# Forward transforms of two of four convolutions in three reduced-precision passes, with x loaded in a second order

## The chip, the cores and the metric

The kernel runs on one core of a Trainium2 chip. The metric is the device time of one execution in microseconds; the time before is the median of three runs. A core has five engines, each of which takes its instructions in order: TensorE (PE, with its weight loads as PEld), VectorE (DVE), ScalarE (ACT), GpSimd (POOL) and SyncE (SP). SP and POOL also issue transfers (DMA). Engines wait for each other through semaphores.

## The reference

2048 tokens of width D = 576 pass through two residual halves. `sa, ca, ga, sb, cb, gb` are the six parts of a modulation computed from a condition vector.

```python
h = _layernorm(x, axis=-1) * (1 + ca) + sa
x = x + ga * _A_ref(h, ...)          # long convolution along the tokens
h = _layernorm(x, axis=-1) * (1 + cb) + sb
x = x + gb * (relu(h @ w1) @ w2)     # w1: 576 x 4608, w2: 4608 x 576
```

`_A_ref` builds a convolution kernel K of 2048 steps for each of the 576 channels from 128 complex exponentials, convolves h with it by way of a Fourier transform, and adds `h * D_skip`. All inputs and outputs are float32.

## The kernel before

**Segments and blocks.** The tokens are cut into four segments of 512, s = 0 to 3. For each segment the kernel runs a convolution `conv(s)` and then a block of the feed-forward layer, block b = s. A block has 36 steps g of 128 hidden columns; over the kernel g counts from 0 to 143. One g is `first` (L1368, 14 matmuls of 128x512 into `hps`), the relu and its split on ScalarE and VectorE (`hh` at L1373, `hl` at L1374), and `second` (L1394, 14 matmuls into five `acc` tiles). These matmuls are in three passes over high and low parts: operands are fp32r, a float32 of reduced precision, and each product is high by high, high by low and low by high. `hh` and `xh` are high parts, `hl` and `xl` low parts; the weights are split the same way (L1333, L1343).

**Interleaving.** `conv(s+1)` is a generator that is advanced while block s runs: block 1 (g = 36 to 71) carries the last part of the convolution kernel's generation (`kps` at L521, evicted to `ker` at L531) and then conv(2); block 2 (g = 72 to 107) carries the end of block 1's output and conv(3). `step` (L1534) is called in the middle of every `first` and `second` and takes from the generator until the work done, in estimated microseconds, reaches a target that rises by `rate(b)` a call (L1706), with at most 7.0 in four calls and at most two matmul groups in one. A scheduler then fixes the order on every engine, and `Kept` marks instructions that stay in program order.

**A convolution.** conv(s) loads x of its segment (`x2`, four tokens in each partition, partition m holding tokens 4m to 4m+3), normalises it into `h` (`norm1`, L925: eight statistics on VectorE at L903, four aggregations at L912, four square roots on ScalarE at L913, then two VectorE operations a quarter at L937 and L938), and loads the kernel rows `kt` in two halves p. `mm_K(p)` and `mm_U(p)` are the first step of the forward transforms of kernel and input: `transform` (L845) makes eight fp32 matmuls of 128x128 by 128x288 each (`ps_f`, L854) with a table of cosines and sines as stationary operand, and evicts each on ScalarE (L855, `Z`). In conv(1) to conv(3) `ps_f` has one PSUM buffer. Butterflies on VectorE (L868 to L882) finish the transform; products with the spectra of earlier segments (L1034 to L1040), an inverse transform (L1061) and the addition to `x2` (L1066) follow. There are two tables because the kernel rows lie in another order: `fcK` has row j for position 8(j mod 16) + floor(j/16), `fcU` has row j for position j. conv(1) to conv(3) each have 32 `ps_f`.

**Transfers.** x, kt, the spectra (`Ua`, `Ka`, `R`) and the output's stores go by POOL's queue; the weights and the kernel rows' stores by SP's. Tiles called `S` (seven buffers) hold spectra, `h` and intermediate results; tiles called `T` (two buffers) hold half of one.

Of the kernel before, what the change touches and what calls it, by code (L numbers as in the profile page):

```python
# [18 lines left out]
P = 128  # L19
L = 2048  # L20
D = 576
# [8 lines left out]
PC = 288  # L30
# [21 lines left out]
class KGen:  # L52
# [10 lines left out]
    def v(self, out, a, b, op):  # L63
        self.tc.keep_in_program_order(self.nc.vector.tensor_tensor(out, a, b, op=op))  # L64
# [511 lines left out]
class Body:  # L576
# [34 lines left out]
    def early(self, kg):  # L611

        nc, I, sm = self.nc, self.I, self.sm
        x2 = self.x2[0] = self.x2p[0].tile([P, 4, D], F32, tag="x2", bufs=1, name="x2_0")
        nc.sync.dma_start(out=x2, in_=I["x"][0:512, :].rearrange("(m n) d -> m n d", n=4))
        self.fcU, self.fcK, self.gc = (
            sm.tile([P, 4, 2, P], F32, name=n) for n in ("fcU", "fcK", "gc")
        )
        for t, n in ((self.fcK, "fck"), (self.fcU, "fcu"), (self.gc, "gc")):
            nc.sync.dma_start(out=t, in_=I[n])  # L620
        kept = self.tc.keep_in_program_order
        self.mv1 = mv = sm.tile([P, 4, 5], F32, name="mv1")
        for i in range(4):
            yield
            st = sm.tile([P, 2, 6], F32, tag="st", bufs=8, name="st0")
            for p in range(2):
                kept(nc.vector.bn_stats(out=st[:, p], in_=x2[:, i, p * PC : (p + 1) * PC]))
            kept(nc.vector.bn_aggr(out=mv[:, i, 0:2], in_=st))
        yield
        kept(nc.scalar.activation(mv[:, :, 2], mv[:, :, 1], AF.Sqrt, bias=self.eps))  # L630
# [310 lines left out]
    def conv(self, s):  # L941

        nc = self.nc
        v = self.vec.tensor_tensor
        xp = self.xp[s % 2]
        if s:
            x2 = self.x2p[s % 2].tile([P, 4, D], F32, tag="x2", bufs=1, name=f"x2_{s}")
            self.x2[s] = x2
            Kept(self.tc, nc.gpsimd).dma_start(
                out=x2,  # L950
                in_=self.I["x"][s * 512 : (s + 1) * 512, :].rearrange("(m n) d -> m n d", n=4),
            )
        else:
            x2, h = self.x2[0], self.h0
            self.fcKn, self.gcn = (
                self.cv.tile([P, 4, P], F32, name=n) for n in ("fcKn", "gcn")
            )
            for t, a in zip((self.fcKn, self.gcn), self.I["neg"]):
                nc.gpsimd.dma_start(out=t, in_=a)
# [4 lines left out]

        kt = [kernel_tile(0) if s else self.kt0, None]
        yield -1 if s else "mod"
        if s:
            h = self.spec(f"h_{s}").rearrange("p a b c -> p a (b c)")
        hv = h.rearrange("m n (dd p q) -> m n dd p q", dd=4, p=2)

        def mm_U(p, Z):
            return self.transform(lambda n2: hv[:, n2, :, p], self.fcU, Z, s == 0)

        def mm_K(p, Z):
            ktv = kt[p].rearrange("p (t dd g) q -> p t dd g q", t=2, g=2)
            if s == 0 and p == 1:
                self.skip(kt[p], p, Kept(self.tc, nc.gpsimd))
            src = lambda n2: ktv[:, n2 // 2, :, n2 % 2]
            if s == 0 and p == 1:
                return self.transform1(src, self.fcK, self.fcKn, Z)  # L980
            return self.transform(src, self.fcK, Z, s == 0)
# [112 lines left out]
            yield from mm_K(1, ZK)  # L1094
            self.save(self.Rd[0][0], Ks[0], Kept(self.tc, nc.gpsimd))
        else:
            yield from both(self.norm1(x2, h), mm_K(0, ZK))
            kt[1] = kernel_tile(1)
            ZU = self.spec("Z")
            yield from both(spec_K(0, ZK), mm_U(0, ZU))  # L1100
# [603 lines left out]
            yield  # L1704

    def rate(self, b):  # L1706
        return (2.15, 1.8, 1.4, 0.5)[b]


def after(n, g):  # L1710
# [6 lines left out]
def both(a, b):  # L1717

    while True:
        n = 0  # L1720
        for g in (a, b):
            for w in g:
                n = 1
                yield w
                break
        if not n:
            return
# [62 lines left out]
```

## Time and profile before

| | |
|---|---|
| median of three runs | 1320.32 us (1318.6 to 1320.47) |
| the profiled execution | 1324.17 us, span 1322.4 us |
| mean granted TensorE clock | 0.943 |
| TensorE matmuls busy | 1210.1 us, 92% of the span |
| VectorE busy | 993.3 us, 75% |
| ScalarE busy | 518.8 us, 39% |
| GpSimd busy | 161.1 us, 12% |
| matmuls `ps_f` at L854 | 240 records, 80.2 us |
| chain of waits | PE 71%, DVE 16%, DMA 7% |

Busy times are summed over instructions of an engine, where overlaps count once. In the groups, "x128" is a count, "mean ns" the time of one. Matmuls are pipelined, so a matmul's record is longer than the distance to the next one's start; the cost of one in a run of many is read from the starts. An fp32 matmul of L854 appears as two records. "[2.69 <-ACT ker L531]" behind a row means that the engine was idle for 2.69 us before it and what released it. The clock is the part of full speed that was granted to TensorE.

### The profile page before, as it was taken

The page shows a single profiled execution, that of the slowest core. Times are in us where ns is not written, and L with a number is a line of the kernel's source. Part 1 is how long each engine was busy: PE and PEld are TensorE (multiplying, and loading weights), DVE is VectorE, ACT ScalarE, POOL GpSimd, SP SyncE. Part 2 cuts the span into 40 slices and gives each one's busy share as a digit, 9 for nine tenths or more (in the row PEclk, how much of TensorE's full clock was granted, in tenths as well). Part 3 has the DMA queues.
Part 4 walks back from the last instruction along what each step waited for, and adds up shares of the span by engine and source line. Part 5 has one row for each costly group of instructions (what it writes and reads, how often), then busy time and mean ns, then how long its engine had stood idle before and what let it go on. Part 6 is the DMA issues. An engine that isn't in the chain of part 4 may idle for free.

```text
span 1322.4 us, 27077 instructions
## 1 busy us (share of the span) xinstructions
PE 1210.1 (92%) x11094; PEld 973.6 (74%) x11094; DVE 993.3 (75%) x1538; ACT 518.8 (39%) x902; POOL 161.1 (12%) x256
## 2 busy tenths in 40 slices
PE   4665586899989998999999999999999999999998
PEld 3454464677767787787677887887888888998997
DVE  7899988999986999689468995467997237555543
ACT  5788423222223422622243225433222365434431
POOL 1676411011000100110001000100000000000000
PEclk9556787999989999999899999999999999999999
DMA  9758972988878967799779995877996658666641
GB/s 273 269 201 307 327 275 79 351 289 321 312 267 294 344 228 274 249 405 343 251 266 340 348 353 155 274 220 263 373 388 191 180 166 256 190 190 190 193 142 63
DMA packets 118032, 343.81 MB, mean 260 GB/s; under 512 B 17772, under 2 KB 21652, under 8 KB 107156
## 3 DMA queue, kind: packets, MB, share of 16 engines
q1 hardware_dynamic: 101332, 226.04, 51.0%
q0 software_dynamic: 16064, 114.67, 22.9%
q8 instruction: 87, 1.43, 0.4%
q10 hardware_dynamic: 512, 1.38, 0.3%
q14 instruction: 37, 0.30, 0.1%
HBM read 260.63 MB, written 81.40 MB: 259 GB/s over the span
## 4 chain that ended last, share of the span: by engine, by line
PE 71%; DVE 16%; DMA 7%; issue 3%; ACT 1%; POOL 1%; SPq 0%; ACTq 0%; DVEq 0%
PE acc L1394 28%; PE hps L1368 21%; PE hps L1495 7%; PE ps_f L854 5%; DMA L1d<-w 4%; PE kps L73 2%; PE kps L521 2%; PE ps_i L1061 2%; PE ph L73 2%; DVE T L486 1%; DVE W1r L488 1%; DMA x<-in_x_dram 1%; DVE Y L1040 1%; DVE T L64 1%; DVE w L1338 1%
## 5 line engine op out<-in xcount | busy, mean ns | idle before, releaser
L1394 PE MATMUL acc<-w,hh 128*128 128x512 f32 x1008 | 323.1, 403 | 3.2 <-ACT hh L1373 2.7
L1368 PE MATMUL hps<-xh,w 128*128 128x512 f32 x880 | 307.4, 410 | 0.7 <-ACT xh L49 0.7
L1394 PEld LDWEIGHTS acc<-w,hh 128*128 128x128 f32 x1008 | 187.4, 188 | 44.0 <-ACT hh L1373 3.6
L1368 PEld LDWEIGHTS hps<-xh,w 128*128 128x128 f32 x880 | 168.6, 192 | 38.7 <-ACT xh L49 1.3
L1394 PE MATMUL acc<-w,hl 128*128 128x512 f32 x504 | 195.1, 401 | 1.5 <-DVE hl L1374 1.5
L1343 ACT ACTIVATE w<-r 128x576 fp32r<-128x576 f32 x141 | 96.6, 685 | 229.7 <-PE acc L1394 195.2
L1368 PE MATMUL hps<-xl,w 128*128 128x512 f32 x440 | 175.7, 400 | 0.0
L1373 ACT ACTIVATE hh<-hps 128x512 fp32r<-128x512 f32 x110 | 65.7, 597 | 242.1 <-PE hps L1368 237.4
L1374 DVE SCALAR_TENSOR_TENSOR hl<-hps,hh 128x512 fp32r<-128x512 f32 x110 | 75.4, 685 | 113.1 <-ACT hh L1373 112.5
L1394 PEld LDWEIGHTS acc<-w,hl 128*128 128x128 f32 x504 | 94.3, 189 | 22.8 <-DVE hl L1374 3.0
L1333 ACT ACTIVATE w<-r 128x640 fp32r<-128x640 f32 x124 | 90.8, 732 | 42.7 <-DMA L1d<-w 42.1
L1368 PEld LDWEIGHTS hps<-xl,w 128*128 128x128 f32 x440 | 84.1, 191 | 18.3 <-DVE xl L49 0.4
L1040 DVE TENSOR_TENSOR Y<-Y,T 128x1152 f32<-128x1152 f32 x60 | 79.3, 1348 | 0.0
L73 PE MATMUL kps<-W,W 128*32 128x16 f32 x2304 | 39.4, 210 | 42.8 <-POOL W L70 28.4
L1368 PE MATMUL hps<-xs,w 128*128 128x512 f32 x220 | 78.0, 421 | 0.0
L855 ACT ACTIVATE Z<-ps_f 128x288 f32<-128x288 f32 x120 | 49.0, 410 | 71.6 <-PE ps_f L854 69.7
L73 PEld LDWEIGHTS kps<-W,W 128*32 128x32 f32 x2304 | 34.7, 142 | 56.4 <-POOL W L70 31.0
L521 PEld LDWEIGHTS kps<-W1r,W2r 128*32 128x32 f32 x3456 | 45.1, 113 | 38.8 <-issue 20.8
L521 PE MATMUL kps<-W1r,W2r 128*32 128x48 f32 (+2 forms) x3456 | 52.4, 202 | 15.9 <-ACT ker L531 9.3
L1503 DVE TENSOR_TENSOR C<-C,hps 128x256 f32<-128x256 f32 x17 | 7.1, 420 | 63.0 <-PE hps L1495 63.0
L1394 PE MATMUL acc<-hh,w 128*128 128x512 f32 x126 | 50.7, 402 | 0.0
L1394 PE MATMUL acc<-hl,w 128*128 128x512 f32 x126 | 49.9, 396 | 0.0
(307 smaller groups left out, 2197.9 us busy)
## 6 DMA issues: line engine op xcount, KB each, us to landing
r<-in_w_dram SPq DMA_DIRECT2D x144, 320.0 KB, 3.9
r<-in_w_dram SPq DMA_DIRECT2D x144, 288.0 KB, 4.9
w<-L2d SPq DMA_DIRECT2D x108, 288.0 KB, 4.1
w<-L1d SPq DMA_DIRECT2D x92, 320.0 KB, 3.9
W2r<-W2d POOLq DMA_DIRECT2D x18, 1536.0 KB, 8.5
W2d<-W SPq DMA_DIRECT2D x12, 1536.0 KB, 8.5
Ua<-Ud POOLq DMA_DIRECT2D x15, 1152.0 KB, 9.5
W<-W1d POOLq DMA_DIRECT2D x18, 768.0 KB, 9.4
```

The lines of the kernel that those rows point to most:

```text
L73: self.tc.keep_in_program_order(self.nc.tensor.matmul(*args, **kw))
L521: nc.tensor.matmul(ps[32 * dd : 32 * dd + 32, q, :], W2[:, r, ch], W1[:, r, ch], start=(r == 0), stop=(r == 1),)
L854: nc.tensor.matmul(o, fc[:, n2, c, :], src(n2), start=True, stop=True)
L855: ev = nc.scalar.activation(Z[:, n2, c], ps[:, :PC], AF.Copy)
L1040: v(y, y, T, op=op or ALU.add)
L1333: copy(g - 1)(w1[g][:, 0], r1[g], AF.Copy)
L1343: copy(g)(w[:, 0:D], r2[g], AF.Copy)
L1368: nc.tensor.matmul(ps, a, x, start=(i == 0), stop=(i == 13))
L1373: nc.scalar.activation(hh, ps, AF.Relu)
L1374: nc.vector.scalar_tensor_tensor(hl, ps, 0.0, hh, op0=ALU.max, op1=ALU.subtract)
L1394: nc.tensor.matmul(acc[i], a, x, start=(f == 0 and seen[i] == 1), stop=(f == NF - 1 and seen[i] == (3 if i < 4 else 2)),)
L1495: nc.tensor.matmul(out, l, m, start=(i == 0), stop=(i == len(ops) - 1))
```

## The change

For s = 2 and 3 the first step of the forward transforms is done by a new function `thirds` in place of `transform`. It splits its source into a high part (copy to fp32r on ScalarE, two of 128x576) and a low part (subtraction on VectorE, two of 128x576), in `T` tiles, and makes each `ps_f` from three fp32r matmuls: table high by source high, table high by source low, table low by source high. `table`, run once at s = 2, splits `fcK` in the same way; the high part takes the buffer of `fcU`, the low part that of `fcK`. One table then serves both transforms, because x to be normalised (`h`) is now loaded in the kernel rows' order, straight into the tile in which it is normalised. x in the natural order is needed for the residual and is loaded a second time, after `norm1` and the first kernel transform. The targets of blocks 1 and 2 in `rate` are raised. conv(0) and conv(1) compute as before.

```diff
-        if s:
+        def load_x():
             x2 = self.x2p[s % 2].tile([P, 4, D], F32, tag="x2", bufs=1, name=f"x2_{s}")
...
+        def load_h():
+            h = self.spec(f"h_{s}").rearrange("p a b c -> p a (b c)")
+            Kept(self.tc, nc.gpsimd).dma_start(
+                out=h.rearrange("m n d -> m (n d)"),
+                in_=bass.AP(
+                    tensor=self.I["x"].tensor, offset=self.I["x"].offset + s * 512 * D,
+                    ap=[[4 * D, 8], [32 * D, 16], [1, 4 * D]],
+                ),
+            )
+            return h
+
+        if s == 1:
+            x2 = load_x()
+        elif s:
+            h = load_h()
...
+        def split(x, name):
+            hi, lo = (
+                self.half(name + n).rearrange("p n (a b) -> p n a b", a=4).bitcast(F32R)
+                for n in "hl"
+            )
+            for i in range(2):
+                h, l = (t[:, 2 * i : 2 * i + 2] for t in (hi, lo))
+                nc.scalar.activation(h, x[i], AF.Copy)
+                v(l, x[i], h, op=ALU.subtract)
+                yield 0.8
+            return lambda n2: (hi[:, n2], lo[:, n2])
+
+        def table():
+            f = lambda t: t.rearrange("p n c k -> p (n c k)")
+            sm, shape = self.sm, [P, 4, 2, P]
+            hi = sm.tile(shape, F32R, tag="fcU", bufs=1, name="fch")
+            nc.scalar.activation(f(hi), f(self.fcK), AF.Copy)
+            t = self.spec("fct").rearrange("p a b c -> p (a b c)")[:, :1024]
+            v(t, f(self.fcK), f(hi), op=ALU.subtract)
+            yield 1.5
+            lo = sm.tile(shape, F32R, tag="fcK", bufs=1, name="fcl")
+            nc.scalar.activation(f(lo), t, AF.Copy)
+            self.parts = hi, lo
+
+        def thirds(p, Z, x, name):
+            hi, lo = self.parts
+            src = yield from split(x, name)
+            for n2 in (0, 2, 1, 3):
+                xh, xl = src(n2)
+                for c in range(2):
+                    ps = self.cps.tile([P, 512], F32, tag="cps", bufs=self.nps, name="ps_f")
+                    o = ps[:, :PC].rearrange("p (a b) -> p a b", a=4)
+                    fh, fl = hi[:, n2, c], lo[:, n2, c]
+                    for i, (a, b) in enumerate(((fh, xh), (fh, xl), (fl, xh))):
+                        nc.tensor.matmul(o, a, b, start=(i == 0), stop=(i == 2))
+                    nc.scalar.activation(Z[:, n2, c], ps[:, :PC], AF.Copy)
+                    yield None
...
-            yield from both(self.norm1(x2, h), mm_K(0, ZK))
+            if s == 2:
+                yield from table()
+            yield from both(self.norm1(h if s > 1 else x2, h), mm_K(0, ZK))
+            if s > 1:
+                x2 = load_x()
...
-        return (2.15, 1.8, 1.4, 0.5)[b]
+        return (2.15, 1.86, 1.46, 0.5)[b]
```

Behind the change the line numbers move: `first` and `second` are at L1432 and L1458, `hh` and `hl` at L1437 and L1438, the matmuls of `thirds` at L1022 with their eviction at L1023, the split at L995 and L996, the table at L1006 and L1009.

Three places in the order of the engines follow. The first is VectorE at the start of conv(2), from the kernel generation's last multiplications (`W1r_11`) on; `st1` are the statistics, `mv` their aggregation, and the three `hl` are those of g = 48, 49 and 50. Before:

```order
L490 TENSOR_TENSOR W1r_11_7422<-W1r_11_7422,T_7514 128x48x16
L492 TENSOR_TENSOR W1r_11_7422<-W1r_11_7422,T_7514 128x48x16
L903 BN_STATS st1_7762<-x2_2_7739 128x6
L903 BN_STATS st1_7763<-x2_2_7739 128x6
L903 BN_STATS st1_7764<-x2_2_7739 128x6
L903 BN_STATS st1_7765<-x2_2_7739 128x6
L903 BN_STATS st1_7762<-x2_2_7739 128x6
L903 BN_STATS st1_7763<-x2_2_7739 128x6
L1374 SCALAR_TENSOR_TENSOR hl_7571<-hps_7528,hh_7570 128x512
L903 BN_STATS st1_7764<-x2_2_7739 128x6
L903 BN_STATS st1_7765<-x2_2_7739 128x6
L912 BN_AGGR mv_7841<-st1_7762 128x2
```

and in the changed kernel:

```order
L490 TENSOR_TENSOR W1r_11_7422<-W1r_11_7422,T_7514 128x48x16
L492 TENSOR_TENSOR W1r_11_7422<-W1r_11_7422,T_7514 128x48x16
L1438 SCALAR_TENSOR_TENSOR hl_7571<-hps_7528,hh_7570 128x512
L1438 SCALAR_TENSOR_TENSOR hl_7751<-hps_7723,hh_7750 128x512
L1006 TENSOR_TENSOR fct_7763<-fcK_284,fch_7761 128x1024
L1438 SCALAR_TENSOR_TENSOR hl_7849<-hps_7821,hh_7848 128x512
L903 BN_STATS st1_7767<-h_2_7739 128x6
L903 BN_STATS st1_7768<-h_2_7739 128x6
```

The statistics, six of which stood ahead of the first `hl` behind the kernel generation's last rows in the old order, now stand behind three of them and behind the table's subtraction, and they read the tile `h_2`.

The second is ScalarE at the same place; `ker` is the eviction (L531) of the kernel generation's matmuls, L913 are the square roots. Before:

```order
L1373 ACTIVATE hh_7570<-hps_7528 128x512
L1333 ACTIVATE w1_7578<-r1_7425 128x640
L531 ACTIVATE ker_6_6732<-kps_7536 128x32x6
L913 ACTIVATE mv_7841<-mv_7841,eps_206 128x1
L913 ACTIVATE mv_7844<-mv_7844,eps_206 128x1
L913 ACTIVATE mv_7847<-mv_7847,eps_206 128x1
L913 ACTIVATE mv_7850<-mv_7850,eps_206 128x1
L531 ACTIVATE ker_6_6732<-kps_7605 128x32x6
L1343 ACTIVATE w2_7754<-r2_7427 128x576
L531 ACTIVATE ker_6_6732<-kps_7662 128x32x6
```

and in the changed kernel, up to the first eviction of `hh` behind the last `ker`:

```order
L1437 ACTIVATE hh_7570<-hps_7528 128x512
L1397 ACTIVATE w1_7578<-r1_7425 128x640
L531 ACTIVATE ker_6_6732<-kps_7536 128x32x6
L531 ACTIVATE ker_6_6732<-kps_7605 128x32x6
L1407 ACTIVATE w2_7754<-r2_7427 128x576
L531 ACTIVATE ker_6_6732<-kps_7662 128x32x6
L1437 ACTIVATE hh_7750<-hps_7723 128x512
```

The four square roots, which stood between two `ker` evictions, stand behind all of them now, behind three further `hh` (not all shown).

The third is the start of conv(3). POOL's queue before, with the stores of block 1's output, the load of x and that of a spectrum:

```order
L841 DMA Ka_8696<-Kd_1_1_118 128x2304
L841 DMA Ua_8698<-Ud_1_1_104 128x2304
L1669 DMA out_0_dram<-x2_1_5203 128x576 x4
L49 DMA x2_3_9264<-in_x_dram 128x2304
L841 DMA R_9466<-Rd_2_0_113 128x2304
L1291 DMA kt_9463<-kd_3_1_64 128x16x72
```

and in the changed kernel:

```order
L841 DMA Ua_8800<-Ud_1_1_104 128x2304
L1355 DMA kt_9588<-kd_3_1_64 128x16x72
L1733 DMA out_0_dram<-x2_1_5203 128x576 x4
L49 DMA h_3_9347<-in_x_dram 128x1x2304
L49 DMA x2_3_9586<-in_x_dram 128x2304
L841 DMA R_9591<-Rd_2_0_113 128x2304
```

The load of `h_3` stands where that of `x2_3` stood, and the load of `x2_3` is behind it. The old load of x wrote the tile from which the stores read; `h_3` is another tile. kt of the second half has moved ahead of the stores. ScalarE there, before:

```order
L855 ACTIVATE Z_9276<-ps_f_9327 128x288
L855 ACTIVATE Z_9276<-ps_f_9338 128x288
L1343 ACTIVATE w2_9399<-r2_9217 128x576
L855 ACTIVATE Z_9276<-ps_f_9349 128x288
L913 ACTIVATE mv_9368<-mv_9368,eps_206 128x1
L913 ACTIVATE mv_9371<-mv_9371,eps_206 128x1
L913 ACTIVATE mv_9374<-mv_9374,eps_206 128x1
L913 ACTIVATE mv_9377<-mv_9377,eps_206 128x1
L855 ACTIVATE Z_9276<-ps_f_9365 128x288
```

and in the changed kernel:

```order
L1023 ACTIVATE Z_9363<-ps_f_9425 128x288
L1397 ACTIVATE w1_9422<-r1_9310 128x640
L1023 ACTIVATE Z_9363<-ps_f_9438 128x288
L913 ACTIVATE mv_9474<-mv_9474,eps_206 128x1
L913 ACTIVATE mv_9477<-mv_9477,eps_206 128x1
L913 ACTIVATE mv_9480<-mv_9480,eps_206 128x1
L1023 ACTIVATE Z_9363<-ps_f_9451 128x288
L913 ACTIVATE mv_9483<-mv_9483,eps_206 128x1
L1407 ACTIVATE w2_9505<-r2_9312 128x576
L1023 ACTIVATE Z_9363<-ps_f_9457 128x288
```

Before, the square roots (L913) stood ahead of the eviction of the last `ps_f` of this transform. Now they stand ahead of that of the fifth, `ps_f_9451`, and three more `ps_f` follow on TensorE, which wait for the one buffer.

More of the change, by code (lines that the diff above doesn't have):

```diff
@@ L616, in early @@
         self.fcU, self.fcK, self.gc = (
-            sm.tile([P, 4, 2, P], F32, name=n) for n in ("fcU", "fcK", "gc")
+            sm.tile([P, 4, 2, P], F32, tag=n, bufs=1, name=n) for n in ("fcU", "fcK", "gc")
         )
@@ L952, in conv @@
             )
+            return x2
+        def load_h():
[12 more added lines that the diff above has]
+            h = load_h()
         else:
@@ L966, in conv @@
         yield -1 if s else "mod"
-        if s:
+        if s == 1:
             h = self.spec(f"h_{s}").rearrange("p a b c -> p a (b c)")
         hv = h.rearrange("m n (dd p q) -> m n dd p q", dd=4, p=2)
+        def split(x, name):
[33 more added lines that the diff above has]
+                    yield None
         def mm_U(p, Z):
+            if s > 1:
+                return thirds(p, Z, [hv[:, 2 * i : 2 * i + 2, :, p] for i in range(2)], "hs")
             return self.transform(lambda n2: hv[:, n2, :, p], self.fcU, Z, s == 0)
@@ L977, in mm_K @@
                 self.skip(kt[p], p, Kept(self.tc, nc.gpsimd))
+            if s > 1:
+                x = kt[p].rearrange("p (t dd g) q -> p t g dd q", t=2, g=2)
+                return thirds(p, Z, [x[:, i] for i in range(2)], "ks")
             src = lambda n2: ktv[:, n2 // 2, :, n2 % 2]
@@ L1096, in conv @@
         else:
-            yield from both(self.norm1(x2, h), mm_K(0, ZK))
+            if s == 2:
+                yield from table()
+            yield from both(self.norm1(h if s > 1 else x2, h), mm_K(0, ZK))
+            if s > 1:
+                x2 = load_x()
             kt[1] = kernel_tile(1)
```

## The prediction

> **What bounds the kernel now.** I read the busy line and the clock line of the page first, then a table of windows, then the chain of waits, then the timeline where the chain leaves TensorE. The windows (columns: busy of PE, PEld, DVE, ACT, POOL, then granted clock, DMA share, GB/s) cover the last two convolutions, s=2 from about 630 us and s=3 from about 840 us.
>
> ```profile
> 630.00:642.00 12.00, 12.00 (x192) 9.04 (x194) 9.06 (x8) 2.26 (x4) 2.12 (x3) 1.00 0.96 339
> 642.00:660.00 18.00, 15.31 (x279) 11.63 (x279) 5.52 (x22) 4.78 (x12) 0.54 (x1) 0.81 0.62 200
> 660.00:846.00 186.00, 186.00 (x815) 148.65 (x813) 133.22 (x183) 73.18 (x134) 13.09 (x22) 1.00 0.82 287
> 860.00:1010.00 150.00, 150.00 (x650) 121.42 (x650) 129.00 (x146) 48.93 (x87) 7.97 (x15) 1.00 0.83 296
> ```
>
> From 660 us on TensorE is busy in all of the time at a clock of 1.00, so there a change is worth what it takes off TensorE, as long as no wait is put in. One window is different: 642 to 660, with 2.69 us without TensorE and a clock of 0.81. The timeline shows its cause and its price:
>
> ```profile
> 630.40 0.53 POOL L49 DMA_DIRECT2D x<-in_x_dram  x1
> ...
> 644.49 2.26 DVE L903 BATCH_NORM_STATS2 st<-x 128x6 f32<-128x288 f32 x6 [5.33 <-DMA x<-in_x_dram]
> ...
> 648.20 0.85 ACT L913 ACTIVATE mv<-mv,eps 128x1 f32<-128x1 f32 x4 [4.72 <-DVE mv L912]
> ...
> 649.33 0.95 PE L521 MATMUL kps<-W1r,W2r 128*32 128x32 f32 x48 [2.69 <-ACT ker L531]
> ```
> ```profile
> 650.00:656.00 6.00, 6.00 (x78) 4.47 (x69) 0.00 (x0) 1.03 (x2) 0.54 (x1) 0.54 0.41 113
> ```
>
> VectorE stands for 5.33 us before x of segment 2, issued at 630.40. The statistics end in four square roots on ScalarE, ScalarE takes its work in order, and behind the roots stands the eviction (L531) that TensorE's next kernel matmuls need. TensorE loses 2.69 us, which is all of the 18.00 - 15.31 in that window, and afterwards runs six microseconds at 0.54 of its clock, another 6 x 0.46 = 2.8 us: 5.5 us in all.
>
> **The transforms.** 64 `ps_f` of s=2 and 3 change; each is one fp32 matmul that the trace records twice. What one costs I take from starts:
>
> ```profile
> 885.80 0.65 PE L854 MATMUL ps_f<-h,fcU 128*128 128x288 f32 x2
> ...
> 887.91 0.65 PE L854 MATMUL ps_f<-h,fcU 128*128 128x288 f32 x2
> ```
> ```profile
> 1149.27 0.40 PE L1495 MATMUL hps<-Th,S 128*128 128x256 f32 x2
> ...
> 1154.26 0.62 PE L1394 MATMUL acc<-w,hh 128*128 128x512 f32 x2
> ...
> 1156.78 0.39 PE L1394 MATMUL acc<-w,hl 128*128 128x512 f32 x1
> ```
> ```profile
> 675.30 0.73 PE L854 MATMUL ps_f<-kt,fcK 128*128 128x288 f32 x2
> ...
> 680.32 0.72 PE L854 MATMUL ps_f<-h,fcU 128*128 128x288 f32 x2
> ```
>
> In the second fence, 42 matmuls of 128x256 start between the first two rows, 4.99 us, 0.119 each; 11 of 128x512 between the last two, 2.52 us, 0.229 each. In the first, one `ps_f` and seven matmuls of 128x512 fill the 2.11 us: 2.11 - 7 x 0.229 = 0.51 us for the `ps_f`. In the third, a dense stretch, four of them with three matmuls of 128x512 behind each take 5.02 us, 1.255 each: 0.57 for the `ps_f`, because the one PSUM buffer has to be evicted (0.41 us on ScalarE) first. A reduced-precision matmul of 288 columns lies on the line between the rows of 256 and 512: 0.119 + 32/256 x 0.110 = 0.133, three of them 0.40 us, and with the same surplus of up to 0.03 at the change of kind 0.40 to 0.43. So 0.08 to 0.11 us saved by each, 5.1 to 7.0 us on 64. The planner's steeper targets for s=2 and 3 (1.86, 1.46) put more of them at the dense distance, where each costs 0.06 more: some ten, -0.6. I take **-5 us**. Ends by the nearest rows: at 256 columns' price 3 x 0.119 gives -10; at 512 columns' price 3 x 0.229 gives +11. 288 lies next to 256, so the second end is far out.
>
> By the Trainium skill (FP8 and Floating Point Precision, TensorE Precision Notes) true fp32 is four passes through the array, so three would save a quarter, an estimate of 0.49/4 = 0.12 us each or 7.8 us. The trace's two records for one fp32 matmul neither confirm nor refute a four.
>
> **What has to run for it.** Per convolution eight 128x576 copies on ScalarE and eight 128x576 subtractions on VectorE, and once two copies and one subtraction of 1024 columns.
>
> ```profile
> L1343 ACT ACTIVATE w<-r 128x576 fp32r<-128x576 f32 x141 | 96.6, 685 | 229.7 <-PE acc L1394 195.2
> L868 DVE TENSOR_TENSOR W<-Z x24: 745/751/759, 426.5 to 957.0; 128x576 f32<-128x576 f32 x24
> L1457 ACT ACTIVATE S<-Sr x17: 1042/1062/1062, 1094.2 to 1278.3; 128x1024 fp32r<-128x1024 f32 x17
> L1458 DVE TENSOR_TENSOR S<-Sr,S x17: 1218/1228/1229, 1095.8 to 1279.4; 128x1024 fp32r<-128x1024 f32 x17
> ```
>
> ScalarE: 8 x 0.685 = 5.5 us per convolution, plus 2.1 once; it was busy 73 of 186 us. VectorE: 8 x 0.751 = 6.0, plus 1.2 once; it has 53 idle of 186 and 21 idle of 150, so on average there is room, and I cost it at nothing on the path. The cover is thin in places:
>
> ```profile
> 720.00:740.00 20.00, 20.00 (x88) 16.25 (x87) 19.72 (x18) 6.17 (x12) 2.25 (x3) 1.00 1.02 384
> 920.00:940.00 20.00, 20.00 (x88) 16.12 (x88) 19.82 (x17) 5.83 (x12) 1.22 (x3) 1.00 1.03 412
> ```
>
> Here VectorE is full and TensorE still waits for nothing, since `hl` is made about one g (28 matmuls of 0.229 us, 6.4 us) ahead of its use. If that lead runs out, the 6 us come onto the path. For the later end of convolution 2 (its last transposes come about one g later, close to the next block's first matmuls) I add **+0.5** (0 to 1).
>
> **Segment 2's start.** In the new order h_2's statistics stand behind `hl` of g=48, 49 and 50, not inside g=48's work, and the square roots behind all L531 evictions. h_2 may be issued about a microsecond later (it waits for the multiplication that reads W0_11 last), but its statistics come about two g, some 12 us, later than before. So the stall at 649 and the slow clock behind it go, and from 630 to 642, with the same kernel matmuls but no roots, TensorE waited for nothing: **-5.5 us** (0 if h_2 were as late again). kt of s=2 now waits for the last kernel matmul, at about 649 on the old clock, and its first reader stands about 2.5 g, 16 to 17 us, behind that. Its landing in the trace took less, column us to landing, though little less:
>
> ```profile
> kt<-kd POOLq DMA_DIRECT2D x1, 576.0 KB, 14.7
> ```
>
> The second load of x (1152 KB) is needed only at the residual, tens of us later: nothing.
>
> **Segment 3's start.** Before, x was issued after the stores of the output had landed:
>
> ```profile
> 840.06 1.14 POOL L1669 DMA_DIRECT2D out_dram<-x  x2 [0.71 <-DVE x L1667]
> 846.19 0.54 POOL L49 DMA_DIRECT2D x<-in_x_dram  x1 [4.99 <-DMA out_dram<-x]
> ...
> 853.21 2.98 DVE L903 BATCH_NORM_STATS2 st<-x 128x6 f32<-128x288 f32 x8 [3.47 <-DMA x<-in_x_dram]
> ...
> 856.33 0.86 ACT L913 ACTIVATE mv<-mv,eps 128x1 f32<-128x1 f32 x4 [2.73 <-DVE mv L912]
> ```
>
> VectorE and ScalarE waited there, but in the old order nothing that TensorE needed was behind them. Now h_3 is issued at about 841.2, right behind the stores. Its first four statistics stand ahead of `hl` of one g, and the square roots ahead of a `ps_f` eviction that TensorE needs, by the order and the matmul prices, at about 852. From landing to that eviction's end: eight statistics 2.98, one `hl` 0.7, aggregation and roots up to 0.9, eviction 0.4: 5.0 us. h_3 must land by 847.0, 5.8 us after issue. x of segment 3 took 853.2 - 846.2 = 7.0 us, x of segment 2 644.5 - 630.4 = 14.1. Beside the stores in the same queue 7.0 gives 848.2; all behind them, 846.2 + 7.0 = 853.2. I take 849, nearer the first because the stores had been under way since 838, a stall of **+2 us** (0 if it lands by 847, 6 at 853.2). A stall as long as the 2.69 at 649 would bring the slow clock too, 2.8 more.
>
> By the Trainium skill (TensorE: Matmul & The Clock Gate, Part 1) the clock falls after an idle window of about 3.4 us. The row here shows a fall at 2.69 idle; by the page a 3 us stall would stay 3, by the row it becomes near 6.
>
> **Sum.** -5 - 5.5 + 2 + 0.5 = -8.0 us. It is made against the profiled execution: span 1322.4 (1324.17 with what lies around it), so 1314.4 and 1316.2 after. The median of the runs is 1320.32, about 4 less than that execution; with the same difference the median becomes **1312.3 us**.
>
> **Rivals.**
> - *The stall only moves.* h_3 lands at about 851 to 852, TensorE waits 4 to 5 us for the roots and runs slowly afterwards: 5 + 2.8 instead of 2, net -2.2, **1318.1**. For it: the 14.1 us of segment 2's x. Against: segment 3's 7.0.
> - *No new stall and more off the transforms.* h_3 lands by 847, and each `ps_f` saves what the dense rows allow, 0.57 - 0.45 = 0.12: -7.7 - 5.5 + 0.5 = -12.7, **1307.6**. For it: most of the transforms of s=2 stand at the dense distance. The Trainium skill's quarter (FP8 and Floating Point Precision) comes to the same.
> - *The transforms give nothing*, since the eviction of the one buffer sets the pace: -5.5 + 2 + 0.5 = -3.0, **1317.3**. For it: 0.41 us of eviction behind each, and ScalarE has 5.5 us of copies more. Against: at seven matmuls' distance no eviction is waited for.
> - *VectorE becomes the bound* (the slower side). Its place is 700 to 760 and 900 to 1000, where it is full already. If nothing of its 6.0 + 1.2 and 6.0 us is hidden and TensorE's saving there becomes idle, the time goes by -5.5 + 13.2 = +7.7, to **1328**; with half of it hidden 1321.4. It decides once less than about half is hidden, when `hl` comes later than the matmuls that read it. Against: 53 and 21 us idle in the two stretches.
> - *The change doesn't do what it says* at segment 2: h_2 still comes late and only the transforms gain; that needs a landing over 25 us, and I give it nothing of its own.
>
> **How the numbers follow.** Forecast 0.45, the stall moves 0.20, the fast rival 0.13, transforms give nothing 0.12, VectorE 0.10. 0.2% is 2.6 us, about what a measurement can tell from none. Faster: 0.45 + 0.13 + 0.11 + half of 0.20 = 0.79; same: the other half, and 0.01 each of the last two = 0.12; slower: the rest, 0.09. The likeliest case's own range is 1308.5 to 1316 (transforms -2 to -7, new stall 0 to 5). For 8 in 10: down to 1306, below which only the 256-column price lies, and up to 1320, which leaves out VectorE's case and the worst of the moved stall.
>
> **What would show it.** Right: no wait at L903 or L531 near 640 to 650 and a clock of 1.00 there; `ps_f` three records 0.13 apart, about 0.43 us in sum; a wait of ScalarE for L912 near 842 to 850 with a TensorE idle of about 2 us behind a `ps_f` eviction. Wrong: TensorE waiting for `hl` at 700 to 760 or 900 to 1000; idle time in front of the first `ps_f` of s=2 (kt late); a clock under 1.00 anywhere behind 640.

## The result, and the profile after

The changed kernel takes 1330.72 us (median of six runs, 1328.73 to 1333.16); the kernel before, run beside it, 1317.71 (1314.38 to 1320.47). The ratio is 1.0091, with a 95% interval from 1.0063 to 1.0119: 0.9% slower. The forecast was 1312.3, with a range up to 1320.

The two profiled executions had already parted by 4.7 us before the first instruction that the change moves, in work that is the same in both: the second half of g = 36 began at 556.54 us before and at 551.85 after. From there to the last matmul the kernel before took 760.8 us and the changed one 772.3: +11.5 us, close to the 13.0 us between the medians. All sums below count from g = 36.

The windows of the changed kernel, with the columns of those shown for before (busy of PE, PEld, DVE, ACT, POOL, granted clock, DMA share, GB/s):

```profile
642.00:660.00 18.00, 17.24 (x164) 13.83 (x165) 5.15 (x11) 6.07 (x10) 2.30 (x3) 1.00 0.92 290
720.00:740.00 20.00, 20.00 (x90) 16.56 (x89) 20.00 (x18) 6.04 (x10) 0.53 (x1) 1.00 0.97 366
740.00:760.00 20.00, 20.00 (x89) 16.40 (x88) 20.00 (x31) 5.44 (x9) 1.31 (x3) 1.00 0.78 256
780.00:800.00 20.00, 19.02 (x82) 15.07 (x82) 20.00 (x21) 6.33 (x11) 0.00 (x0) 1.00 0.80 279
838.00:854.00 16.00, 7.02 (x36) 5.62 (x34) 0.00 (x0) 2.35 (x5) 1.09 (x2) 0.87 1.03 185
860.00:864.00 4.00, 4.00 (x13) 3.26 (x12) 3.47 (x6) 0.55 (x2) 0.00 (x0) 0.55 0.46 165
```

Segment 2's start is nearly mended: 0.76 us without TensorE where there were 2.69, and a clock of 1.00. The loss is in the fifth row. Over 16 us VectorE did nothing, TensorE worked 7.02 us, and the DMA engines were busy all of the time and yet moved only 185 GB/s. The timeline names what was waited for:

```profile
832.93 1.14 POOL L1733 DMA_DIRECT2D out_dram<-x  x2 [0.71 <-DVE x L1731]
834.07 0.64 POOL L49 DMA_DIRECT2D h<-in_x_dram  x1
838.68 0.56 POOL L49 DMA_DIRECT2D x<-in_x_dram  x1 [3.97 <-issue]
...
854.71 1.54 DVE L903 BATCH_NORM_STATS2 st<-h 128x6 f32<-128x288 f32 x4 [20.66 <-DMA h<-in_x_dram]
...
858.42 0.67 ACT L913 ACTIVATE mv<-mv,eps 128x1 f32<-128x1 f32 x3 [15.67 <-DVE mv L912]
859.00 0.39 ACT L1023 ACTIVATE Z<-ps_f 128x288 f32<-128x288 f32 x1
...
859.43 0.61 PE L1022 MATMUL ps_f<-ksh,fch 128*128 128x288 f32 x1 [14.42 <-ACT Z L1023]
```

This is the chain that the prediction described, link by link: the load of h_3, four statistics, `hl`, four statistics, the square roots, the eviction that stands behind them, the next `ps_f`. From landing (854.68) to the eviction's end it took 4.7 us, against the 5.0 estimated. But h_3 landed 20.6 us after its issue, where the prediction took 7.8 (issue at 841.2, landing at 849), and TensorE stood for 14.42 us. For four microseconds afterwards it ran at 0.55 of its clock.

What each stretch of g took, less its matmuls at the measured price of each kind, gives this account (worked out from the starts of the matmuls in both traces, which give 0.490 us for an fp32 `ps_f` and 0.133 for one of its three matmuls now; us, after less before):

```
transform matmuls, 64 x (0.490 - 3 x 0.133)        -5.8
g = 36 to 46                                       +0.6
g = 47 (the stall at segment 2)                    -4.2
g = 48 to 55 (evictions and weights, s = 2)        +2.2
g = 66 to 71 (hl late, end of s = 2)               +1.8
g = 73 (h_3)                                      +16.4
all the rest                                       +0.5
sum                                               +11.5
```

The waits of TensorE from 560 to 1100 us, in the view that groups them (line waited for: us in total, times, longest), show the same place:

```profile
PE ps_f L1022 <- ACT Z L1023: 14.4, 1, 14.4
PE acc L1458 <- DVE hl L1438: 1.0, 2, 0.5
PE kps L521 <- issue: 1.0, 2, 0.8
PE hps L1432 <- DMA w<-L1d: 0.6, 1, 0.6
```

### The profile page after: what moved, and what is told of

The parts are those of the page before. It is cut to its first block, busy times and chain, and to the rows that moved or that the text cites. A ratio compares the mean times of both kernels' runs of the same rounds, so it can differ in the third digit from the quotient of the medians.

```text
span 1329.2 us, 27259 instructions
## 1 busy us (share of the span) xinstructions
PE 1201.5 (90%) x11158; PEld 969.4 (73%) x11158; DVE 1000.0 (75%) x1555; ACT 529.6 (40%) x920; POOL 161.5 (12%) x258
## 4 chain that ended last, share of the span: by engine, by line
PE 66%; DVE 16%; DMA 9%; issue 4%; POOL 1%; ACT 1%; SPq 0%; DVEq 0%; ACTq 0%; POOLq 0%
PE acc L1458 26%; PE hps L1432 19%; PE hps L1559 7%; PE kps L521 3%; DVE T L1098 3%; PE ps_f L854 2%; DVE Y L1100 2%; PE kps L73 2%; DMA L1d<-w 2%; DMA w<-L1d 2%; PE ps_f L1022 2%; DMA Ua<-Ud 2%; PE ph L73 2%; DMA h<-in_x_dram 2%; PE ps_i L1121 1%
## 5 line engine op out<-in xcount | busy, mean ns | idle before, releaser
L1458 PE MATMUL acc<-w,hh 128*128 128x512 f32 x1008 | 317.4, 397 | 4.6 <-ACT hh L1437 3.1
L1432 PE MATMUL hps<-xh,w 128*128 128x512 f32 x880 | 301.5, 402 | 0.7 <-ACT xh L49 0.7
L1458 PEld LDWEIGHTS acc<-w,hh 128*128 128x128 f32 x1008 | 186.2, 188 | 42.9 <-ACT hh L1437 4.0
L1458 PE MATMUL acc<-w,hl 128*128 128x512 f32 x504 | 192.7, 398 | 2.5 <-DVE hl L1438 2.5
L1432 PEld LDWEIGHTS hps<-xh,w 128*128 128x128 f32 x880 | 166.8, 191 | 36.0 <-ACT xh L49 1.3
L1432 PE MATMUL hps<-xl,w 128*128 128x512 f32 x440 | 174.7, 398 | 0.1
L1437 ACT ACTIVATE hh<-hps 128x512 fp32r<-128x512 f32 x110 | 65.7, 597 | 239.4 <-PE hps L1432 232.2
L1438 DVE SCALAR_TENSOR_TENSOR hl<-hps,hh 128x512 fp32r<-128x512 f32 x110 | 75.3, 685 | 97.5 <-ACT hh L1437 97.3
L1458 PEld LDWEIGHTS acc<-w,hl 128*128 128x128 f32 x504 | 93.6, 188 | 23.6 <-DVE hl L1438 5.3
L1432 PEld LDWEIGHTS hps<-xl,w 128*128 128x128 f32 x440 | 83.6, 190 | 18.0 <-DVE xl L49 0.6
L1432 PE MATMUL hps<-xs,w 128*128 128x512 f32 x220 | 75.1, 408 | 0.6 <-DMA w<-L1d 0.6
L521 PEld LDWEIGHTS kps<-W1r,W2r 128*32 128x32 f32 x3456 | 44.5, 111 | 38.5 <-issue 24.7
L521 PE MATMUL kps<-W1r,W2r 128*32 128x48 f32 (+2 forms) x3456 | 52.2, 199 | 15.5 <-issue 9.3
L1458 PE MATMUL acc<-hh,w 128*128 128x512 f32 x126 | 50.3, 399 | 0.0
L1458 PE MATMUL acc<-hl,w 128*128 128x512 f32 x126 | 49.7, 395 | 0.0
L486 DVE TENSOR_TENSOR T<-W,Zr 128x1536 f32<-128x1536 f32 x24 | 42.0, 1748 | 9.4 <-DMA Zr<-Zd 9.3
```

Source lines behind the costliest of these rows:

```text
L486: v(T, X, zi, op=ALU.mult)
L521: nc.tensor.matmul(ps[32 * dd : 32 * dd + 32, q, :], W2[:, r, ch], W1[:, r, ch], start=(r == 0), stop=(r == 1),)
L1432: nc.tensor.matmul(ps, a, x, start=(i == 0), stop=(i == 13))
L1437: nc.scalar.activation(hh, ps, AF.Relu)
L1438: nc.vector.scalar_tensor_tensor(hl, ps, 0.0, hh, op0=ALU.max, op1=ALU.subtract)
L1458: nc.tensor.matmul(acc[i], a, x, start=(f == 0 and seen[i] == 1), stop=(f == NF - 1 and seen[i] == (3 if i < 4 else 2)),)
```

## The experiments

Two questions stood: why does h_3 take 20 us, and what would the change be worth if it didn't? On the first, theory P was that the order of the rows is slow by itself; theory Q that x and R, now put on the queue 5 us behind h_3, shared its bandwidth. On the second, theory S was that the whole loss is the place of the square roots ahead of an eviction.

**The order of rows alone.** A kernel of nothing but loads of 1152 KB, one at a time, in the orders of this access pattern (`a` groups, each of rows that lie `a` apart; 8 is the change's). Lines of that kernel, in which `R` is 4 * D and `g` issues on POOL's queue:

```diff
+            def pat(s, a, b, eng=g):
+                return lambda t: eng.dma_start(out=t, in_=src(s, [[R, a], [a * R, b], [1, R]]))
...
+                one(f"nat{s}", lambda t: g.dma_start(out=t, in_=src(s, [[R, 128], [1, R]])))
+                one(f"a8s{s}", pat(s, 8, 16))
+                one(f"a16s{s}", pat(s, 16, 8))
+                one(f"a4s{s}", pat(s, 4, 32))
+                one(f"a2s{s}", pat(s, 2, 64))
```

> This kernel computes nothing: it loads 512 rows of x (1152 KB) over and over into one tile, each load alone, and writes x's first segment out. The loads differ only in the order in which packets of 9216 bytes are read: natural, rows 2, 4, 8 or 16 apart in turn (8 is the changed kernel's), the 8-apart order as 16 transfers that read in address order and write every 16th partition, the same as four transfers of 2304-byte packets, and two loads issued by SP. Theory P (the order of reading is slow by itself): natural lands in 4 to 7 us, 8 apart in at least 1.7 times that with packets of 0.6 us or more instead of 0.35, and reading in address order is near natural. Theory Q (only the company of the second x and R in the queue made the 20 us): all orders within 20% of each other, packets near 0.35 us.

The DMA issues of that kernel (KB each, median us to landing):

```profile
nat<-in_x_dram POOLq DMA_DIRECT2D x2, 1152.0 KB, 5.5
a8s<-in_x_dram POOLq DMA_DIRECT2D x2, 1152.0 KB, 12.8
a16s<-in_x_dram POOLq DMA_DIRECT2D x2, 1152.0 KB, 7.9
a4s<-in_x_dram POOLq DMA_DIRECT2D x2, 1152.0 KB, 20.4
a2s<-in_x_dram POOLq DMA_DIRECT2D x2, 1152.0 KB, 25.0
rows<-in_x_dram POOLq DMA_DIRECT2D x32, 72.0 KB, 3.6
cols<-in_x_dram POOLq DMA_DIRECT2D x8, 288.0 KB, 5.8
```

Alone, too, the change's order takes 12.8 us against 5.5: theory P holds in that, and the main cause is seen in the packets. Their summed durations, divided by the time from the first to the last, give how many were under way at once:

```
order (outermost dim)   packets x mean us   at once   landing us
natural (128)               128 x 0.42        14.0        5.5
16 groups                   128 x 0.64        14.2        7.9
 8 groups (the change)      128 x 0.64         7.8       12.8
 4 groups                   128 x 0.55         3.7       20.4
 2 groups                   128 x 0.37         2.0       25.0
```

Up to 16, as many packets were under way as the outermost dimension of the access pattern has entries: the 8 groups of the change keep 8 of the 16 DMA engines at work. The Trainium skill (DMA: Bandwidth & Descriptors, "Why a DMA increments its semaphore by 16 and not by 1") states just that: the number of engines is the largest up to 16 that divides the slowest dimension of both sides. The five rows agree with it. Four transfers of quarter rows (`cols`), one behind the other, kept 12.5 busy, and the last had landed 8.4 and 8.0 us after the first issue.

Beside this a packet of the reordered loads took 0.64 us instead of 0.42 (8 and 16 groups). Reading in address order did not shorten them: the sixteen transfers that read in address order (`rows`) had packets as long (0.71 and 0.61 us in the two repetitions), 9.8 and 8.7 of them at once, and were complete 11.5 us after the first issue, of which POOL's issuing alone takes 8.3. "Near natural", as theory P had it, they were not. In the changed kernel, from 838 to 854 us, packets of 9216 bytes (those of h_3, x and R together) took 0.63 to 0.94, and 0.35 to 0.36 once h_3 had landed. What makes them longer stays open.

**The changed kernel with natural rows.** Only the order of the load is changed.

```diff
-                    ap=[[4 * D, 8], [32 * D, 16], [1, 4 * D]],
+                    ap=[[4 * D, 128], [1, 4 * D]],
```

> The changed kernel with h_2 and h_3 loaded in natural order and nothing else touched (the order on every engine is the same); x's transforms in segments 2 and 3 then use the wrong rows of the table. Theory P: h_3 lands in 7 to 10 us instead of 20.6, the 14.4 us without TensorE at 845 become 1 to 4, and the time falls by 10 to 16 us, to 1315 to 1320. Theory Q: x and R still stand 5 us behind in the queue, h_3 still takes 15 us or more, and the time stays above 1325.

1321.5 us median (ratio to before 1.0023, 0.9998 to 1.0047). The time falls by about 9 us against the change, a little less than expected, and the issues give the reason (KB each, us to landing), with the wait that is left:

```profile
h<-in_x_dram POOLq DMA_DIRECT2D x1, 1152.0 KB, 9.9
x<-in_x_dram POOLq DMA_DIRECT2D x1, 1152.0 KB, 8.6
R<-Rd POOLq DMA_DIRECT2D x1, 1152.0 KB, 11.7
```
```profile
PE ps_f L1022 <- ACT Z L1023: 3.7, 1, 3.7
```

x and R stand where they stood, 5 us behind, and h_3 lands in 9.9: theory Q falls. TensorE still waits 3.7 us at the same `ps_f`, and runs at half its clock for 3.4 us behind it; g = 73 takes 13.6 us, 5.3 more than in the run below where h_3 comes early (8.3). So with a landing inside the prediction's bounds this term lies inside its range too (0 to 6), though near the upper end and not at 2.

**The normalisation later.** In segment 3 the normalisation is written behind the eight transforms of the first kernel half.

```diff
+            if s == 3:
+                yield from mm_K(0, ZK)
+                yield from self.norm1(h, h)
+            else:
                 yield from both(self.norm1(h if s > 1 else x2, h), mm_K(0, ZK))
```

> The changed kernel, but in segment 3 the normalisation comes behind all eight transforms of the first kernel half instead of being interleaved with them; the load keeps its order of rows. Theory S (the loss is the place of the square roots ahead of an eviction, so a late h_3 costs only there): with some 14 us more until h_3 is needed TensorE waits 0 to 3 us near 845 to 865, and the time falls to 1313 to 1320. If instead TensorE would have stood for h_3 anyway (its transforms come just behind), the wait only moves some g later and the time stays above 1325.

1331.4 us (ratio 1.0083, 1.0062 to 1.0105): nothing gained, the second of the two outcomes expected. TensorE's wait is now ended by VectorE instead of ScalarE. This is TensorE's timeline of that kernel:

```profile
847.06 0.61 PE L1462 MATMUL acc<-w,hh 128*128 128x512 f32 x2
856.45 0.80 PE L1462 MATMUL acc<-w,hl 128*128 128x512 f32 x1 [8.78 <-DVE hl L1442]
```

The scheduler set the statistics ahead of an `hl` on VectorE, and TensorE waits 8.78 us for that. (The profiled execution took 1323.94 us, the shortest of the ten; what the others lost was not seen.) Theory S, that only the place of the roots costs, is too narrow: whatever stands behind a statistic of h_3 waits for h_3.

**Read in address order.** Sixteen transfers of eight adjacent rows, each writing every 16th partition.

```diff
...
+            for b in range(16):
+                Kept(self.tc, nc.gpsimd).dma_start(out=f[b::16], in_=x[8 * b : 8 * b + 8])
...
```

> The changed kernel with each h loaded by 16 transfers: each reads eight rows that lie next to each other and writes every 16th partition, so the same h arrives, read in address order. Theory P, if it is the order of the reads: h_3's rows land in 8 to 13 us from the first issue (16 issues of about 0.55 us each on POOL take 8.8 themselves), the wait at 845 falls to 2 to 7 us and the time to 1317 to 1324. If the order of the writes over partitions is what is slow, or Q holds: 20 us and above 1328.

1378.02 us (1.0435, 1.0394 to 1.0476). Neither expected outcome came. With 32 transfers in place of two the order on all engines is another one, and the largest wait, 34.5 us of TensorE for `hl` in four places, stands beside loads of spectra that come late (POOL issued R at 799.33, after standing 10.67 us for VectorE). The time tells nothing of the order of reading.

**h_3 early.** The load of h is no longer held in program order, so that the scheduler may place it; h_3 then stands ahead of the stores. All else is the change.

```diff
-            Kept(self.tc, nc.gpsimd).dma_start(
+            nc.gpsimd.dma_start(
                 out=h.rearrange("m n d -> m (n d)"),
```

> The changed kernel, with the load of h no longer held to its place in the program: h_3 now stands ahead of the four stores in POOL's queue, which waited some 24 us for them. Its order of rows stays. If the whole loss is that h_3 comes too late for the place of its statistics and roots: h_3 is issued near 808 instead of 834, lands near 830, the 14.4 us at 845 and the slow clock behind them go, and the time falls by 14 to 18 us, to 1312 to 1317. If the slow order of rows also hurts through the weights' transfers that run beside it: TensorE waits for weights near 810 to 835 for 1 to 5 us, and the time ends at 1317 to 1322.

1319.2 us (0.9991, 0.9961 to 1.002). h_3 is issued at 809.84 instead of 834.07, still takes 19.2 us, and lands before anything needs it; the 14.4 us at `ps_f` are gone and no TensorE wait for weights takes their place:

```profile
PE acc L1458 <- DVE hl L1438: 1.6, 2, 1.2
PE hps L1559 <- DVE C L1570: 0.3, 1, 0.3
```

So the late h_3 costs the change 11.5 us by the two medians, 13 by the two ratios and 18.4 by the two traces from g = 36 on (772.3 against 753.9), and 19.2 us without x and R beside it says again that their company does little. But on the second question the result is the kernel before's time, not 8 us less. It lies in the range expected for weights that come late, though no such wait is there.

**Half rows, and the loads without the three passes.** The first loads each h in two transfers of half a row; the second does this with the fp32 transforms and the old targets, so that only the loads and the one table differ from the kernel before. Both are shown in part.

```diff
+            for i in range(2):
+                nc.gpsimd.dma_start(
+                    out=f[:, 2 * D * i : 2 * D * (i + 1)],
+                    in_=bass.AP(
+                        tensor=x.tensor, offset=x.offset + s * 512 * D + 2 * D * i,
+                        ap=[[4 * D, 8], [32 * D, 16], [1, 2 * D]],
...
```
```diff
         def mm_U(p, Z):
-            if s > 1:
-                return thirds(p, Z, [hv[:, 2 * i : 2 * i + 2, :, p] for i in range(2)], "hs")
-            return self.transform(lambda n2: hv[:, n2, :, p], self.fcU, Z, s == 0)
+            fc = self.fcK if s > 1 else self.fcU
+            return self.transform(lambda n2: hv[:, n2, :, p], fc, Z, s == 0)
...
```

> As the run before, and each h in two transfers of half a row, 4608 bytes. By the load runs one transfer in this order keeps 8 of 16 DMA engines busy; two keep more. Theory P: h_2, alone in the queue, lands in 10 to 14 us instead of 22, and the time is 0 to 2 us under the run before. If the number of transfers doesn't matter: h_2 still lands in 20 us or more, and the two times agree within 0.1%.

> The loads of the run before without the three passes: the transforms of segments 2 and 3 are fp32 as in the kernel before, both with the one table, and the targets are the old ones. It gives the same result. Against the kernel before it shows what the loads alone do (expected: the stall at segment 2 goes, -4 to -5.5 us, 1314 to 1316 where before is at 1319). Against the run before it shows the worth of the three passes: by the prediction 5 us, by the trace of the changed kernel 5.8 us of matmuls less 2 to 4 us of new waits for evictions and for hl, so 2 to 4 us. If the new waits eat all of it, the two agree within 1 us.

Halves: 1318.37 us (1.0001, 0.9971 to 1.0031). From the first issue to the second landing h_2 took 19.6 us and h_3 14.9, where one transfer took 20.4 and 19.2: for h_2 far less gained than the 10 to 14 us expected, and no gain in time over the run before. Loads only: 1321.43 us (1.0021, 0.9992 to 1.0051). The loads alone gain nothing in the median, where 4 to 5.5 us were expected. Between the two medians lie 3 us, and 2.2 from g = 36 on in the traces (756.8 against 759.0 us). That agrees with the 2 to 4 us expected of the three passes, but the targets differ as well and the two intervals overlap, so it is not shown. Both profiles have a new wait at the place of the old stall, with nothing to wait for that the profile shows ("issue"): 1.1 + 1.6 us and 1.3 + 1.4 us (`PE kps L521 <- issue`).

**The kernel before once more.**

> The kernel before, profiled once more. The prediction took 5.5 us for the stall at segment 2 from one execution, which was 4 us longer than the median. If that stall is the same in every execution: 2.5 to 2.9 us without TensorE near 640 to 650 and 6 us at about half clock behind it, 15 us from the second half of g = 47 to that of g = 48. If the execution was an unlucky one: less than 1.5 us, or a clock of 1.00 behind it, 10 to 13 us.

Its second profile, timeline and windows:

```profile
642.61 2.26 DVE L903 BATCH_NORM_STATS2 st<-x 128x6 f32<-128x288 f32 x6 [4.52 <-DMA x<-in_x_dram]
...
647.46 0.72 PE L521 MATMUL kps<-W1r,W2r 128*32 128x32 f32 x48 [1.89 <-ACT ker L531]
```
```profile
650.00:656.00 6.00, 6.00 (x69) 4.94 (x69) 0.31 (x1) 1.97 (x4) 0.54 (x1) 0.83 0.78 227
```

The stall is there, but smaller, between the two cases expected: 1.89 us without TensorE, then 3.4 us at half clock instead of 6.8 (0.83 in that window instead of 0.54), an estimate of 1.89 + 1.7 = 3.6 us where the prediction had 5.5. g = 47 took 13.3 us instead of 15.15, and all from g = 36 on 758.6, 2.2 less than in the first. The 5.5 us of the prediction came from the worse of two executions.

**The old targets, and h_2 in natural order.** Both on top of the run with h_3 early.

```diff
-        return (2.15, 1.86, 1.46, 0.5)[b]
+        return (2.15, 1.8, 1.4, 0.5)[b]
```
```diff
-                    ap=[[4 * D, 8], [32 * D, 16], [1, 4 * D]],
+                    ap=[[4 * D, 8], [32 * D, 16], [1, 4 * D]] if s == 3 else [[4 * D, 128], [1, 4 * D]],
```

> The run with h_3 early (e4), with the old targets 1.8 and 1.4 instead of 1.86 and 1.46: the convolutions are spread over more g, transforms stand less densely and VectorE gets its work later. If the steeper targets cost what the trace shows (2 us of waits for evictions at g = 50 to 55, 1.6 us for hl at g = 66 and 67): 1 to 3.5 us less than e4, about 1316 to 1318. If the end of the convolution, which now comes later, costs as much at the border of the blocks: within 1 us of e4 or above it.

> The run with h_3 early (e4), with h_2 alone loaded in natural order (its transforms then use the wrong rows of the table); the order on every engine is that of e4. It shows whether h_2's slow order costs through its neighbours, as it runs beside the last kernel matmuls, for which the traces show TensorE waiting for nothing but its own instructions. If yes: 1 to 3 us less than e4 in the median, h_2 landing in 7 to 14 us. If no: within 1 us of e4.

Old targets: 1316.35 us (0.9982, 0.9955 to 1.0009); `hl` costs TensorE 0.9 us instead of 1.6. h_2 natural: 1315.29 us (0.997, 0.9943 to 0.9996), 3.9 us under the run with h_3 early, with h_2 landing in 11.2 us instead of 20.4. It is the only version whose interval lies under 1, and it leaves out the right order. The expectation took such a gain as a sign that h_2's load costs through its neighbours. That is not shown: the two intervals overlap, the two kernels were measured on different chips, and their traces from g = 36 on take the same time (754.0 against 753.9 us) with no wait for "issue" in either.

**Quarter rows, and the old targets again.** Both with h_3 early and the old targets, the first with h_2 in four transfers of a quarter row (`q = 4 if s == 2 else 1`).

> The run with h_3 early and the old targets (e10), with h_2 in four transfers of a quarter row each; all of the result is computed. Alone, four such transfers landed in 8.7 us where one took 12.8. If more transfers bring more DMA engines here as well: h_2 lands in 10 to 15 us instead of 21, TensorE does not wait for its own instructions near 640 to 650, and the time is 0 to 2 us under e10 and 3 to 6 us under the kernel before. If the slow packets are the price and not the number of engines: as e10 or above it.

> The run with h_3 early and the old targets (e10) once more, for its interval beside the kernel before on this chip: 0.9955 to 1.0009 there. If its profile (8 us less than the kernel before from g = 36 on, 5.8 less than that kernel's second profile) is typical: a ratio of 0.995 to 0.998 with an interval under 1. If not: an interval with 1 in it.

Quarters: 1317.82 us (0.9978, 0.9957 to 1.0). A quarter landed 13.6 us after its own issue (median of four), but h_2 was complete only 18.0 us after the first, not in the 10 to 15 expected, and TensorE waited 2.0 us for "issue", where no wait was expected. Old targets again: 1319.26 us (0.9997, 0.9978 to 1.0016), an interval with 1 in it, so the first profile of this kernel (1310.63 us, the shortest of its ten executions) was not typical. In the second profile TensorE's waits are these:

```profile
PE kps L521 <- issue: 1.8, 1, 1.8
PE acc L1458 <- DVE hl L1438: 0.7, 3, 0.3
PE ps_i L1121 <- DVE V L875: 0.5, 1, 0.5
```

The first of them was absent in the first profile of the same kernel, which is 2.3 us shorter from g = 36 on (752.8 against 755.1). The quarters, with an interval that touches 1, have the lowest ratio of the versions that compute the right result: some 2 us under the kernel before, if anything.

## Why the prediction was wrong

- **Segment 3's start** is the step that failed, by the size of one term. The mechanism, the place and the chain behind the landing were right (4.7 us against 5.0), and the load was mis-sized: "I take 849", bounded by 853.2; it landed at 854.7 on a clock that by then ran 7 us earlier than the old one. I took the 7.0 and 14.1 us of two loads of the same size for the price of this one, though the diff shows another access pattern: 128 rows before, 8 groups of 16 now. That shape alone takes 12.8 us against 5.5, and 20.6 in the changed kernel, beside the other transfers. From issue to landing that is 12.8 us more than the 7.8 assumed; with the 2 us of stall forecast it makes 14.8, and 14.42 were measured. The whole term of +2 us measured +16.4, the rest being mostly slow clock. Read in natural order it measures 5.3, of which 3.7 are idle.
- **The rival "the stall only moves"** named this outcome with 5 + 2.8 us and a chance of 0.2. Its price rested on the same wrong bound, so neither case reached the other side of no change.
- **The transforms.** The price per matmul was right: the trace shows three records 0.13 us apart, and from one `ps_f` to the next with seven matmuls between 0.42 us for the `ps_f`, where 0.40 to 0.43 was estimated.

```profile
839.74 0.29 PE L1022 MATMUL ps_f<-ksh,fch 128*128 128x288 f32 x1
839.87 0.29 PE L1022 MATMUL ps_f<-ksl,fch 128*128 128x288 f32 x1
840.00 0.29 PE L1022 MATMUL ps_f<-ksh,fcl 128*128 128x288 f32 x1
840.13 0.62 PE L1458 MATMUL acc<-w,hh 128*128 128x512 f32 x2
```

  The term of -5 is -5.8 of matmuls and +2.2 of waits at g = 48 to 55, -3.6; the pair with and without the passes lies 2 to 3 us apart, within the noise and with other targets.
- **Segment 2's start** was right in kind (-4.2 in the traces against -5.5) and too large for the other execution that was profiled: the second profile of the kernel before has 1.9 us less at that place. New waits for "issue" stand there in six of the eleven profiles of changed versions.
- **VectorE.** The rival "VectorE becomes the bound" showed its beginnings: VectorE is full from 720 to 760, and TensorE waits for `hl` at 786 and 794. With 1.8 us instead of 13 it did not decide; that its 1328 comes nearest to the measured 1330.72 is luck. The +0.5 us for the later end of convolution 2 is inside that.
- **What stays open.** The late h_3 is why the change is slower, not why it gains nothing without it. With h_3 early the other terms should have left -5 - 5.5 + 0.5 = -10 us. By the ratio the time is 1.2 us less, and the interval, -5.1 to +2.6 us, leaves out both -10 and the -8 of the forecast. The trace from g = 36 on is 4.7 and 6.9 us shorter than the two of the kernel before; with the old targets too the two traces are 3.5 to 8 us shorter, and the medians only 0.2 to 3.7. Single executions of each of these kernels differ by 8 to 16 us from shortest to longest, and only one of them is profiled per run. Two places where the profiles part can be named. The work ahead of g = 36, the same in all of them, took from 551.0 to 556.5 us. And g = 47, the place of the stall, took 15.2 and 13.3 us before, 9.9 to 10.3 in five profiles of changed versions, 11.0 in the change and 12.0 to 13.1 in the four with 1.8 us or more of "issue" and the change's access pattern: its gain is 5 us in some executions and almost nothing in others. What the longer executions spend the rest on was not seen.

## What to carry to other kernels

A load's time is not its size: before a row of the trace is taken as its price, compare the access patterns, above all how many entries the outermost dimension has, and how many transfers of each kind run beside it. When a load moves ahead of work that an in-order engine does for someone else, ask by how much it may be late and not only by how much it is expected to be, and issue it as early as its buffer allows. A stall read from one profiled execution is one draw; where a term rests on it, its size in a second profile is worth more than a finer reading of the first.

## What was not expected of the hardware

- A transfer with 8 groups in its outermost dimension kept 7.8 DMA engines busy, one with 4 groups 3.7, one with 2 groups 2.0, whether POOL or SP issued it (SP, 8 groups: 7.8; natural 13.9).
- While the reordered rows were read, packets of 9216 bytes, those of x and R among them, took 0.63 to 0.94 us instead of 0.35, and the core moved 185 GB/s at a DMA share of 1.03, where before it moved 407 at a share of 1.00:

```profile
849.00:854.00 5.00, 5.00 (x23) 4.04 (x22) 1.48 (x4) 2.34 (x6) 0.00 (x0) 1.00 1.00 407
```

- In the stretch of many small matmuls (48 of 128x32 in 0.7 us) TensorE stood up to 1.8 us at a time with nothing to wait for that the profile shows ("issue"). That happened while h_2's load in 8 groups was under way, in five of eight profiles with it, and up to 3.6 us with h_2 in sixteen transfers; in neither of the two with h_2 in natural order, and in neither of the kernel before. That the load delays TensorE's instructions, which the page of the profile lists as transfers of their own, fits this; it was not shown by itself.
